# Low parts of the gated unit's activations by a negative copy and an accumulating transfer, and the phases' negated sine taken into a VectorE product

## The chip, the cores and the metric

One core of a Trainium2 chip. The time is device microseconds of one launch. The kernel before was timed in three runs, 730.05 to 732.71 us, median 732.13. Beside these stands one profiled execution, which has the rows quoted here.

Engines: TensorE (PE; its weight loads are PEld), VectorE (DVE), ScalarE (ACT), GpSimd (POOL) and SyncE (SP, which issues transfers). Each runs its own list of instructions in order and waits for the others by semaphores.

## The reference

```python
xn = _layernorm(x)                                  # x: 1 x 2048 x 448
# A: long convolution with a kernel made from the state space
A = -exp(log_A_real) + 1j * A_imag                  # 448 x 256
P = exp((A * dt)[:, :, None] * pos)                 # pos = 0 .. 2047
K = 2.0 * einsum("dn,dnl->dl", C * dt, P).real
y = irfft(rfft(xn, 4096) * rfft(K, 4096)) + xn * D_skip
# B: gated unit
h = sigmoid(xn @ w_gate) * (xn @ w_up)              # 2048 x 1792
out = x + y + h @ w_down
```

## The kernel before

Two generators write the program side by side: `conv()` (the convolution) and `glu()` (the gated unit). A loop at the end of the kernel takes the next piece of whichever is less far along by weights written beside the pieces; a scheduler then settles each engine's order from its own estimate of when each instruction can start, and `tc.high_priority` draws some forward.

**The gated unit.** Products are made in pieces of reduced precision: each operand is a high part and a low part, and three products (high x high, high x low, low x high) give one. `gate` (L694) makes 128 of the 1792 hidden columns for 512 tokens: 11 matmuls into each of two banks `gu` (gate and up), Tanh on ScalarE (`th`, L715), `hf = (th + 1) * up` on VectorE (L718), then the high part `hh` as a cast on ScalarE (L723) and the low part `hl = hf - hh` on VectorE (L725). `hf` has one buffer, `hh` and `hl` six each. After a group of two or three such column blocks, for two blocks of 512 tokens each, the down products `po` (L819) run over the group: `hh x dh`, `hh x dl`, `hl x dh` for each block of columns, nine matmuls a bank in a group of three, and VectorE adds the bank to `acc` (L824).

**The chunks.** `kgen` (L454) makes the convolution's kernel in 56 chunks of 8 channels. The 2048 positions are written as 64 coarse by 32 fine steps, so that the sum over the 256 states becomes a matmul of `Et` (64 steps) and `Ft` (32 steps). For a chunk:

- `ahead` (L527): TensorE makes the phases of both in the bank `tr` (L534); ScalarE makes `S` from it: Abs (L542), Sin (L543), the negated Sin of the coarse half (L544), and the cosines from Abs (L545). The five planes of `S` are sin, cos, -sin of the coarse steps, cos, sin of the fine steps. `S` has two buffers.
- `magnitudes` (L489), once for two chunks: GpSimd makes the powers `me` and `mf` by doubling (L500, L512), 11 products one after the other, in two buffers that VectorE frees.
- VectorE: the upper half of `Et` (L599) from cos and sin, the lower half (L600) from cos and -sin in reversed order, as the mirrored phases, and `Ft` (L601). `Et` has two buffers, `Ft` one.
- TensorE: 32 matmuls into the bank `ko` (L615). After four chunks it is copied to `ks`, and `first_stage` (L548) begins its transform.

GpSimd also makes low parts of down weights (`dl`, L789), and towards the end of the chunks begins transfers of weights (L641, L649).

Of the kernel before, what the change touches and what calls it, by code (L numbers as in the profile page):

```python
# [21 lines left out]
N = 256  # L22
# [4 lines left out]
TWO_PI = 2.0 * math.pi  # L27
# [103 lines left out]
def s4d_glu_kernel(ctx, tc, io):  # L131
# [322 lines left out]
    def kgen(pk):  # L454
# [4 lines left out]
            ("me1", [128, 4 * DC, 64], F32), ("mf1", [128, 4 * DC, 32], F32),  # L459
            ("S1", [128, 5, 2 * DC, 32], F32), ("Et1", [128, 2, 2 * DC, 64], F32),  # L460
            ("Et0", [128, 2, 2 * DC, 64], F32), ("Ft", [128, 2, 2 * DC, 32], F32),
            ("S0", [128, 5, 2 * DC, 32], F32), ("mf0", [128, 4 * DC, 32], F32),
            ("me0", [128, 4 * DC, 64], F32), ("pm0", [128, 12, NCH * 2 * DC], F32),
            ("ph0", [128, 2, N], F32R), ("ph1", [128, 2, N], F32R),
        ]
        tl = {n: pk.tile(sh, dt_, name=n) for n, sh, dt_ in late}


# [58 lines left out]
        def ahead(cn):  # L527


            S = tl[f"S{cn % 2}"]  # L530
            ps = psc[-1].tile([128, 2, 512], F32, name="tr", bufs=1)
            ph = pht[cn // 2 % 2]
            for h in range(2):
                nc.tensor.matmul(  # L534
                    ps[:, h], ph[:, cn % 2, 128 * h : 128 * h + 128], sel, start=True, stop=True
                )
            if cn % 2 == 1 and cn + 3 < NCK:
                phase_load(cn // 2 + 2)
            rows = lambda t: t.rearrange("p c (h e) s -> p h c (e s)", h=2)
            pv = ps.rearrange("p h (c x) -> p h c x", c=2)  # L540
            cs = S[:, 1:4:2]
            nc.scalar.activation(rows(cs), pv, AF.Abs)  # L542
            nc.scalar.activation(rows(S[:, 0:5:4]), pv, AF.Sin, scale=TWO_PI)  # L543
            nc.scalar.activation(rows(S[:, 2:3]), pv[:, :, 0:1], AF.Sin, scale=-TWO_PI)  # L544
            sins[:] = [nc.scalar.activation(cs, cs, AF.Sin, scale=-TWO_PI, bias=hpi)]  # L545
            return S
# [32 lines left out]
        for g in range(NCK // NCH):  # L579
            for c in range(NCH):  # L580
# [18 lines left out]
                v.tensor_tensor(Et[:, :, :, 32:64], two(me[:, :, 32:64]), S[:, 1::-1], ALU.mult)  # L599
                v.tensor_tensor(Et[:, :, :, 0:32], two(me[:, :, 0:32]), S[:, 1:3, :, ::-1], ALU.mult)  # L600
                fts[:] = [v.tensor_tensor(Ft, two(mf), S[:, 3:5], ALU.mult)]  # L601
                if cn + 2 < NCK and c % 2 == 0:
# [43 lines left out]
    def rd_load(f, rd=None, eng=nc.sync):  # L646
        if rd is None:
            rd = pg.tile([128, D], F32, name="rd", bufs=RB)
        eng.dma_start(rd, io["B_w_down"][128 * f : 128 * f + 128])  # L649
        return rd  # L650

    def w_low():
# [41 lines left out]
    def gate(w, xs, to, between=None):  # L694
# [29 lines left out]
        with hp(HP):  # L724
            v.tensor_tensor(hl, hf, hh, ALU.subtract)  # L725
        to.append((hh, hl))
# [307 lines left out]
    def conv():  # L1034
        with tc.tile_pool(name="psk", bufs=1, space=PSUM) as ps_, tc.tile_pool(
# [89 lines left out]
    xq, psc, raws, acl, marks, slots, pqs = list(x_first), [], [], [], [None, None], {}, []  # L1125
    W1s, GGs, act = [], [], []
    gens = [conv(), glu()]
# [42 lines left out]
```

## Time and profile before

| what | us |
|---|---|
| median of the three runs | 732.13 (730.05 to 732.71) |
| the profiled execution: its own time | 725.02 |
| its span, first to last instruction | 723.2 |
| TensorE busy in the span | 676.3 (94%) |
| VectorE busy | 565.1 (78%) |
| ScalarE busy | 420.8 (58%) |
| GpSimd busy | 384.5 (53%) |
| `hl` on VectorE (L725), 56 of them | 51.8 |
| lower half of `Et` on VectorE (L600), 56 | 79.5 |
| negated Sin on ScalarE (L544), 56 | 34.1 |
| cast `hh` on ScalarE (L723), 56 | 35.0 |

A grouped row reads: line, engine, operation, out<-in, shapes, count | busy us in all, mean ns of one | idle us of the engine just before them, and which work ended it. A row of stretches gives for each engine the busy time in it, with the instructions in brackets, then the granted clock of TensorE, the mean busy share of the DMA engines and GB/s. A row of waits reads: who <- for whom: us in all, times, the longest. A row of the order of time reads: start, us, engine, line, operation and in brackets the idle time ahead of it. TensorE's matmuls overlap, so its busy time counts some filling and is not a measure of its peak.

### The profile page before, as it was taken

What the parts mean: (1) busy time and instruction counts of PE and PEld (TensorE: products, weight loads), DVE (VectorE), ACT (ScalarE), POOL (GpSimd) and SP (SyncE); (2) the same over time, 40 slices, a digit from 0 to 9 for tenths busy, and PEclk for the clock granted to TensorE, in tenths of its full rate; (3) what the DMA queues carried; (4) which work ended last, traced back from release to release, by engine and by line L of the source; (5) the groups of instructions that cost most, each with busy time, mean ns of one, the idle gap of its engine ahead of it and who ended that gap; (6) DMA issues with size and microseconds to landing.
All of it is one profiled execution on the core that took longest, in us unless ns stands there. A gap on an engine that the chain in (4) does not pass through costs nothing.

```text
span 723.2 us, 19101 instructions
## 1 busy us (share of the span) xinstructions
PE 676.3 (94%) x7780; PEld 532.4 (74%) x7780; DVE 565.1 (78%) x776; ACT 420.8 (58%) x650; POOL 384.5 (53%) x430
## 2 busy tenths in 40 slices
PE   2998799997998999998999999999999999999996
PEld 1765688786886888655778887888877787777784
DVE  5799996799989999999588988987865555565543
ACT  3646364678687788898398687776742222322320
POOL 2120027699888788789556865776855001441004
PEclk9998999999999999999999999999999999999999
DMA  9946328434414545364853232232269999999745
GB/s 205 232 111 189 94 84 266 159 107 165 151 52 135 187 136 170 106 184 140 255 159 136 61 137 97 69 111 69 74 156 250 278 235 239 247 261 238 177 128 154
DMA packets 92823, 115.72 MB, mean 160 GB/s; under 512 B 12432, under 2 KB 81200, under 8 KB 92480
## 3 DMA queue, kind: packets, MB, share of 16 engines
q1 hardware_dynamic: 83328, 94.03, 47.5%
q10 hardware_dynamic: 6704, 14.51, 6.3%
q0 software_dynamic: 2704, 5.96, 3.4%
q8 instruction: 61, 1.00, 0.6%
q14 instruction: 26, 0.21, 0.1%
HBM read 69.70 MB, written 44.76 MB: 158 GB/s over the span
## 4 chain that ended last, share of the span: by engine, by line
PE 62%; DVE 16%; ACT 8%; DMA 7%; issue 4%; SPq 2%; POOL 1%; ACTq 0%; DVEq 0%; POOLq 0%
PE gu L707 24%; PE po L819 15%; PE sp L905 7%; PE ko L615 6%; PE pv L932 4%; PE tr L534 3%; DVE Et L600 2%; DVE Ft L601 2%; DVE Et L599 2%; DVE hl L725 1%; DMA acc_d<-acc 1%; DVE pm L448 1%; ACT S L545 1%; DMA xe<-in_A_u_dram 1%; DVE wl L762 1%
## 5 line engine op out<-in xcount | busy, mean ns | idle before, releaser
L512 POOL TENSOR_TENSOR me<-me,pm 128x32 f32<-128x32 f32 (+1 forms) x168 | 146.1, 870 | 83.5 <-DVE Et L600 70.8
L512 POOL TENSOR_TENSOR mf<-mf,pm 128x64 f32<-128x64 f32 (+1 forms) x112 | 120.7, 1078 | 4.9
L707 PE MATMUL gu<-xh,wh 128*128 128x512 f32 x336 | 100.7, 406 | 1.4 <-ACT xh L220 1.4
L707 PE MATMUL gu<-xh,wl 128*128 128x512 f32 x336 | 95.4, 391 | 0.0
L707 PE MATMUL gu<-xl,wh 128*128 128x512 f32 x336 | 95.1, 390 | 0.0
L819 PE MATMUL po<-dh,hh 128*128 128x448 f32 x224 | 85.7, 383 | 6.7 <-DVE xr L224 2.6
L599 DVE TENSOR_TENSOR Et<-me,S 128x1024 f32<-128x1024 f32 x56 | 81.7, 1460 | 9.5 <-ACT S L545 7.6
L600 DVE TENSOR_TENSOR Et<-me,S 128x1024 f32<-128x1024 f32 x56 | 79.5, 1419 | 8.4 <-ACT me L525 8.4
L601 DVE TENSOR_TENSOR Ft<-mf,S 128x1024 f32<-128x1024 f32 x56 | 79.4, 1418 | 7.4 <-ACT S L545 4.4
L819 PE MATMUL po<-dl,hh 128*128 128x448 f32 x224 | 83.6, 373 | 0.0
L819 PE MATMUL po<-dh,hl 128*128 128x448 f32 x224 | 82.7, 370 | 0.0
L542 ACT ACTIVATE S<-tr 128x1024 f32<-128x1024 f32 x56 | 57.8, 1032 | 39.7 <-PE tr L534 34.8
L707 PEld LDWEIGHTS gu<-xh,wh 128*128 128x128 f32 x336 | 61.9, 192 | 20.1 <-issue 4.8
L723 ACT CAST hh<-hf 128x512 fp32r<-128x512 f32 x56 | 35.0, 626 | 70.4 <-DVE hf L718 59.4
L615 PEld LDWEIGHTS ko<-Et,Ft 128*32 128x32 f32 x3584 | 55.2, 113 | 26.5 <-issue 16.3
L707 PEld LDWEIGHTS gu<-xh,wl 128*128 128x128 f32 x336 | 62.8, 188 | 14.9 <-DVE pl L308 0.7
L707 PEld LDWEIGHTS gu<-xl,wh 128*128 128x128 f32 x336 | 63.0, 188 | 14.0 <-issue 0.7
L615 PE MATMUL ko<-Et,Ft 128*32 128x64 f32 x3584 | 65.5, 225 | 8.1 <-DVE Et L599 4.6
L718 DVE SCALAR_TENSOR_TENSOR hf<-th,gu 128x512 f32<-128x512 f32 x56 | 38.1, 680 | 37.3 <-PE gu L707 27.8
L545 ACT ACTIVATE S<-S,hpi 128x1024 f32<-128x1024 f32 x56 | 65.5, 1170 | 0.0
L824 DVE SCALAR_TENSOR_TENSOR acc<-po,acc 128x448 f32<-128x448 f32 x80 | 48.4, 615 | 20.0 <-PE po L819 19.9
L725 DVE TENSOR_TENSOR hl<-hf,hh 128x512 fp32r<-128x512 f32 x56 | 51.8, 925 | 12.5 <-ACT hh L723 12.5
(196 smaller groups left out, 1286.4 us busy)
## 6 DMA issues: line engine op xcount, KB each, us to landing
sk_d<-sk ACTq DMA_DIRECT2D x14, 512.0 KB
sx<-x_d SPq DMA_DIRECT2D x32, 224.0 KB
skl<-sk_d SPq DMA_DIRECT2D x16, 448.0 KB
vp<-v_d SPq DMA_DIRECT2D x16, 448.0 KB
v_d<-vt SPq DMA_DIRECT2D x62, 112.0 KB
wt_d<-wh SPq DMA_DIRECT2D x9, 512.0 KB
wt_d<-wl SPq DMA_DIRECT2D x9, 512.0 KB
wl<-wt_d SPq DMA_DIRECT2D x9, 512.0 KB
```

The lines of the kernel that those rows point to most:

```text
L512: ins = nc.gpsimd.tensor_tensor(m[:, :, w + a : 2 * w : n], m[:, :, a:w:n], par(base + i).unsqueeze(2).to_broadcast([128, 4 * DC, w // n]) ...
L542: nc.scalar.activation(rows(cs), pv, AF.Abs)
L545: sins[:] = [nc.scalar.activation(cs, cs, AF.Sin, scale=-TWO_PI, bias=hpi)]
L599: v.tensor_tensor(Et[:, :, :, 32:64], two(me[:, :, 32:64]), S[:, 1::-1], ALU.mult)
L600: v.tensor_tensor(Et[:, :, :, 0:32], two(me[:, :, 0:32]), S[:, 1:3, :, ::-1], ALU.mult)
L601: fts[:] = [v.tensor_tensor(Ft, two(mf), S[:, 3:5], ALU.mult)]
L615: nc.tensor.matmul(ko[32 * j : 32 * j + 32, sl], Ft[:, cc, DC * h + 4 * q + j], Et[:, cc, DC * h + 4 * q + j], start=(k == 0), stop=(k == ...
L707: glu_mm[:] = [nc.tensor.matmul(ps, a_, b_, start=(n == 0), stop=(n == len(mm) - 1))]
L725: v.tensor_tensor(hl, hf, hh, ALU.subtract)
L819: glu_mm[:] = [nc.tensor.matmul(po, a_[:, bs], w_, start=(n == 0), stop=(n == 3 * fc - 1))]
L824: v.scalar_tensor_tensor(acc[:, b], po, 0.5, acc[:, b], ALU.mult, ALU.add)
L905: mm = nc.tensor.matmul(to, tb[:kk, t, 64 * c : 64 * c + 64], rhs, start=True, stop=True, skip_group_check=True,)
```

## The change

Two edits, both of the chunk stage.

**Low parts.** A new function `low` makes `hl` as ScalarE's copy of `hh` times -1, and GpSimd then issues a transfer from `hf` into `hl` that adds: `hl = -hh + hf`. While `kgen` runs (its tile `hf1` is put in the list `hfx`, which is emptied behind it) the gated unit takes this way, for 35 of its 56 blocks; the 21 others keep the subtraction. `hf` then alternates between its own buffer and `hf1`, since the transfer reads it later than VectorE did.

**Phases.** `S` has four planes instead of five: sin, cos of the coarse steps, cos, sin of the fine ones. ScalarE's negated Sin is gone. The lower half of `Et` becomes two instructions of half the size: one product with cos, and one scalar_tensor_tensor, `(me * -1) * sin`.

```diff
-            ("S1", [128, 5, 2 * DC, 32], F32), ("Et1", [128, 2, 2 * DC, 64], F32),
+            ("S1", [128, 4, 2 * DC, 32], F32), ("Et1", [128, 2, 2 * DC, 64], F32),
...
-            ("ph0", [128, 2, N], F32R), ("ph1", [128, 2, N], F32R),
+            ("ph0", [128, 2, N], F32R), ("ph1", [128, 2, N], F32R), ("hf1", [128, 512], F32),
         ]
         tl = {n: pk.tile(sh, dt_, name=n) for n, sh, dt_ in late}
+        hfx.append(tl["hf1"])
...
-            cs = S[:, 1:4:2]
+            cs = S[:, 1:3]
             nc.scalar.activation(rows(cs), pv, AF.Abs)
-            nc.scalar.activation(rows(S[:, 0:5:4]), pv, AF.Sin, scale=TWO_PI)
-            nc.scalar.activation(rows(S[:, 2:3]), pv[:, :, 0:1], AF.Sin, scale=-TWO_PI)
+            nc.scalar.activation(rows(S[:, 0:4:3]), pv, AF.Sin, scale=TWO_PI)
...
-                v.tensor_tensor(Et[:, :, :, 0:32], two(me[:, :, 0:32]), S[:, 1:3, :, ::-1], ALU.mult)
-                fts[:] = [v.tensor_tensor(Ft, two(mf), S[:, 3:5], ALU.mult)]
+                v.tensor_tensor(Et[:, 0, :, 0:32], me[:, :, 0:32], S[:, 1, :, ::-1], ALU.mult)
+                v.scalar_tensor_tensor(Et[:, 1, :, 0:32], me[:, :, 0:32], -1.0, S[:, 0, :, ::-1], ALU.mult, ALU.mult)
+                fts[:] = [v.tensor_tensor(Ft, two(mf), S[:, 2:4], ALU.mult)]
...
+    def low(lo, hi, full):
+
+        nc.scalar.activation(lo, hi, AF.Identity, scale=-1.0)
+        nc.gpsimd.dma_start(lo, full, accum_op=ALU.add)
...
-        hf = pg.tile([128, 512], F32, name="hf", bufs=1)
+        if hfx and len(hfs) % 2:
+            hf = hfx[0]
+        else:
+            hf = pg.tile([128, 512], F32, name="hf", bufs=1)
...
-            v.tensor_tensor(hl, hf, hh, ALU.subtract)
+            if not hfx:
+                v.tensor_tensor(hl, hf, hh, ALU.subtract)
+            else:
+                low(hl, hh, hf)
...
                 yield from kgen(pk)
+                hfx.clear()
```

The scheduler's order shifts with it. In the rows below L599 to L601 are lines of before; after the change `hf` is L727, `Ft` L602, the halves of the lower `Et` L600 and L601, the chunk product L616, the down product L831, GpSimd's products L513 and L501, and the transfer L656.

VectorE at a pair of chunks about a quarter of the way through, before (`hf` and `gu` belong to the gated unit, `pm` are powers for later chunks):

```order
L599 TENSOR_TENSOR Et_1125<-me_1122,S_1124 128x32x32
L600 TENSOR_TENSOR Et_1125<-me_1122,S_1124 128x32x32
L725 TENSOR_TENSOR hl<-hf,hh 128x512
L601 TENSOR_TENSOR Ft<-mf_1123,S_1124 128x1024
L448 SCALAR_TENSOR_TENSOR pm_1180<-pm_1180 128x128
L718 SCALAR_TENSOR_TENSOR hf<-th,gu 128x512
```

and of the change, from the same place:

```order
L600 TENSOR_TENSOR Et_1125<-me_1122,S_1124 128x16x32
L727 SCALAR_TENSOR_TENSOR hf_1134<-th,gu 128x512
L774 TENSOR_TENSOR wl<-wraw,wh 128x1024
L602 TENSOR_TENSOR Ft<-mf_1123,S_1124 128x1024
L448 SCALAR_TENSOR_TENSOR pm_1180<-pm_1180 128x128
L727 SCALAR_TENSOR_TENSOR hf<-th,gu 128x512
L600 TENSOR_TENSOR Et_1126<-me_1130,S_1128 128x16x32
L601 SCALAR_TENSOR_TENSOR Et_1126<-me_1130,S_1128 128x16x32
L599 TENSOR_TENSOR Et_1126<-me_1130,S_1128 128x32x32
```

The subtraction between the products is gone, the lower half of `Et` stands as two rows, and `hf` alternates between `hf` and `hf_1134`, which is `hf1`.

TensorE at the head of that group's down products, before (`po_2962` is the first bank; `ko` with `Et1` is the second chunk of the pair):

```order
L819 MATMUL po_2962<-dh_2832,hl_2825 128x448
L819 MATMUL po_2987<-dh_2401,hh_2393 128x448
...
L819 MATMUL po_3012<-dl_2404,hh_2393 128x448
L615 MATMUL ko_2445<-Et1_1125,Ft_1127 32x64 x32
L625 MATMUL ko_2445<-dm_79,ident_69 128x8
L534 MATMUL tr_2797<-sel_76,ph0_1132 128x512 x2
L819 MATMUL po_3012<-dh_2401,hl_2394 128x448
```

and of the change:

```order
L616 MATMUL ko_2449<-Et1_1125,Ft_1127 32x64 x32
...
L831 MATMUL po_2968<-dl_2840,hh_2828 128x448
L831 MATMUL po_2992<-dh_2405,hh_2396 128x448
L616 MATMUL ko_2870<-Et0_1126,Ft_1127 32x64 x32
L535 MATMUL tr_2904<-sel_76,ph1_1133 128x512 x2
L831 MATMUL po_2968<-dh_2837,hl_2829 128x448
L831 MATMUL po_2992<-dl_2408,hh_2396 128x448
```

The same chunk's product has moved ahead of the whole group of down products, the next chunk's is in among the first of them, and the first use of the last `hl` stands behind it. From chunk 27 of 56 on both orders have nearly the same work of the gated unit behind them again at the same chunk.

GpSimd in the second half of the chunks, of the change (`me1` and `mf1` are the magnitudes of a pair of chunks, `hf_5605` and `hf1_1134` the two blocks of tokens of the group's last columns):

```order
L513 TENSOR_TENSOR mf1_1123<-mf1_1123,pm1_1180 128x32x4
L513 TENSOR_TENSOR me1_1122<-me1_1122,pm1_1180 128x32x16
L513 TENSOR_TENSOR mf1_1123<-mf1_1123,pm1_1180 128x32x8
L513 TENSOR_TENSOR mf1_1123<-mf1_1123,pm1_1180 128x32x16
L656 DMA hl_5608<-hf_5605 128x512
L656 DMA hl_5693<-hf1_1134 128x512
L513 TENSOR_TENSOR me0_1130<-me0_1130,pm0_1131 128x32
```

and TensorE where the first of the two is used:

```order
L616 MATMUL ko_5334<-Et1_1125,Ft_1127 32x64 x32
L626 MATMUL ko_5334<-dm_79,ident_69 128x8
L535 MATMUL tr_5667<-sel_76,ph0_1132 128x512 x2
L713 MATMUL gu_5677<-xh_3868,wh_5497 128x512 x3
...
L831 MATMUL po_5767<-dh_5388,hh_5383 128x448
L831 MATMUL po_5712<-dh_5612,hl_5608 128x448
L616 MATMUL ko_5723<-Et0_1126,Ft_1127 32x64 x32
```

Both transfers stand behind all 11 products of the pair's magnitudes; before, the next chain followed there at once. Between the chunk product `ko_5334` and the first use of `hl_5608` TensorE has the last half of a gate and 12 down products.

More of the change, by code (lines that the diff above doesn't have):

```diff
@@ L459, in kgen @@
             ("me1", [128, 4 * DC, 64], F32), ("mf1", [128, 4 * DC, 32], F32),
-            ("S1", [128, 5, 2 * DC, 32], F32), ("Et1", [128, 2, 2 * DC, 64], F32),
+            ("S1", [128, 4, 2 * DC, 32], F32), ("Et1", [128, 2, 2 * DC, 64], F32),
             ("Et0", [128, 2, 2 * DC, 64], F32), ("Ft", [128, 2, 2 * DC, 32], F32),
-            ("S0", [128, 5, 2 * DC, 32], F32), ("mf0", [128, 4 * DC, 32], F32),
+            ("S0", [128, 4, 2 * DC, 32], F32), ("mf0", [128, 4 * DC, 32], F32),
             ("me0", [128, 4 * DC, 64], F32), ("pm0", [128, 12, NCH * 2 * DC], F32),
-            ("ph0", [128, 2, N], F32R), ("ph1", [128, 2, N], F32R),
+            ("ph0", [128, 2, N], F32R), ("ph1", [128, 2, N], F32R), ("hf1", [128, 512], F32),
         ]
         tl = {n: pk.tile(sh, dt_, name=n) for n, sh, dt_ in late}
+        hfx.append(tl["hf1"])
         pms = [tl["pm0"]]
@@ L1125, in s4d_glu_kernel @@
     xq, psc, raws, acl, marks, slots, pqs = list(x_first), [], [], [], [None, None], {}, []
-    W1s, GGs, act = [], [], []
+    W1s, GGs, act, hfx = [], [], [], []
     gens = [conv(), glu()]
```

## The prediction

> **What bounds the kernel now.** I read the run's span and clock first, then the busy time of the engines by stage, then the grouped rows of VectorE inside the stage that the change touches, then the waits of that stage. The change lies between about 143 and 536 us, where the 56 chunks of the convolution kernel are made beside the gated unit. I cut that stage in two where the picture changes:
>
> ```profile
> core 0: 723.2 us, clock 0.984
> ...
> core 0: us, PE busy (x) PEld busy (x) DVE busy (x) ACT busy (x) POOL busy (x), PEclk, DMA share, GB/s
> 143.00:338.00 195.00, 183.21 (x2753) 143.02 (x2751) 185.43 (x190) 158.41 (x238) 165.79 (x163) 0.97 0.43 136
> 338.00:536.00 198.00, 195.16 (x2957) 159.58 (x2960) 162.71 (x171) 139.76 (x202) 134.82 (x156) 1.00 0.41 126
> ```
>
> In the first stretch VectorE is busy for 185.4 of 195 us, 95%, the highest share of any engine, and TensorE has 11.8 us of idle time. In the second TensorE is busy for 195.2 of 198 us and VectorE has 35 us to spare. So work taken from VectorE can only be worth something in the first stretch, and there never more than TensorE's 11.8 us; in the second TensorE sets the pace, and anything that it waits for is lost in full. What VectorE does in the first stretch, and who waits for it:
>
> ```profile
> L600 DVE TENSOR_TENSOR Et<-me,S 128x1024 f32<-128x1024 f32 x28 | 41.6, 1488 | 2.5 <-ACT me L525 2.5
> L601 DVE TENSOR_TENSOR Ft<-mf,S 128x1024 f32<-128x1024 f32 x27 | 40.4, 1498 | 0.1
> L599 DVE TENSOR_TENSOR Et<-me,S 128x1024 f32<-128x1024 f32 x27 | 39.0, 1443 | 3.7 <-ACT me L525 1.9 <-ACT S L545 1.8
> L725 DVE TENSOR_TENSOR hl<-hf,hh 128x512 fp32r<-128x512 f32 x16 | 18.1, 1128 | 0.0
> ...
> PE ko L615 <- DVE Et L599: 4.6, 2, 2.9
> ...
> PE ko L615 <- DVE Ft L601: 2.5, 3, 1.9
> ```
>
> The three products of a chunk take 121 us of the 185, the 16 subtractions that make low parts take 18.1. TensorE's waits in the chunks' own products are for Et and Ft, as they must be if VectorE paces the stretch.
>
> **The change part by part.** *Low parts leave VectorE.* In the chunks 35 subtractions `hl` go, 16 of them in the first stretch: 18.1 us off VectorE there. *The split of one product.* L600 becomes two instructions of 512 elements, one of them a scalar_tensor_tensor. Neither form, with both inputs in SBUF, stands in the trace; the nearest rows bound them:
>
> ```profile
> L600 DVE TENSOR_TENSOR Et<-me,S x56: 1208/1222/2175, 139.1 to 530.4; 128x1024 f32<-128x1024 f32 x56
> L725 DVE TENSOR_TENSOR hl<-hf,hh x56: 623/692/2662, 29.8 to 691.3; 128x512 fp32r<-128x512 f32 x56
> L718 DVE SCALAR_TENSOR_TENSOR hf<-th,gu x56: 628/680/689, 27.5 to 689.9; 128x512 f32<-128x512 f32 x56
> L544 ACT ACTIVATE S<-tr x56: 592/605/670, 135.7 to 527.6; 128x512 f32<-128x512 f32 x56
> L723 ACT CAST hh<-hf x56: 603/621/690, 28.2 to 690.6; 128x512 fp32r<-128x512 f32 x56
> ```
>
> (The three numbers are the least, the median and the most, in ns.) Two halves at the medians, 692 + 680 = 1372 ns against 1222, cost 0.15 us more a chunk: the low end. If each half met what a subtraction met in this stretch, 2 x 1128 against 1488, it is 0.77 us: the high end. A 1024-element product here has a mean 0.27 us above its median, so an operation more should meet about that much more: I take 0.15 + 0.27 = 0.42 us, which lies between. Over 28 chunks that is 11.8 us (ends 4.2 and 21.6). VectorE's net in the first stretch is 11.8 - 18.1 = -6.3 us (ends -13.9 and +3.5).
>
> *ScalarE.* It loses L544, 28 x 0.605 = 16.9 us in the first stretch, and gains 16 negative copies, priced by the cast of the same shape at 0.62 us: 9.9. Net -7 us of its 158. VectorE's idle time put down to ScalarE in the rows above is 2.5 + 3.7 = 6.2 us; ends are nothing and all of it, and I take a third, -2, because most of it is behind the squares (L525), which the change leaves as they are.
>
> *What of it reaches the time.* VectorE's 8.3 us: ends are none (TensorE takes over) and all of it. I take 0.8, because TensorE's 11.8 us of idle time must also cover its waits for ScalarE and the late operands below: -6.6 us. The program's new order fits this. It places chunk products ahead of the down products of their group, so VectorE is asked for Et and Ft earlier and TensorE's other work fills the end of the stretch; the work itself is the same.
>
> *The transfers.* Each is issued by GpSimd, in order, between the magnitude products. Their price on GpSimd is that of its other issues; how long one takes to land is not in the trace for a transfer within SBUF that adds, so the nearest rows bound it:
>
> ```profile
> L643 POOL DMA_DIRECT2D wraw<-in_B_w_up_dram x10 | 5.3, 530 | 0.0
> L641 POOL DMA_DIRECT2D wraw<-in_B_w_gate_dram x5 | 3.9, 788 | 2.0 <-POOL dl L796 1.2 <-ACT x L690 0.8
> ```
> ```profile
> rdw<-in_B_w_down_dram POOLq DMA_DIRECT2D x5, 224.0 KB, 5.2
> ...
> sel<-in_c_sel_dram POOLq DMA_DIRECT2D x1, 256.0 KB, 11.3
> ...
> bk<-in_c_bk_dram POOLq DMA_DIRECT2D x1, 128.0 KB, 2.3
> ```
> ```profile
> POOL me L512 <- DVE Et L600: 22.9, 11, 3.3
> ```
> The first two rows are issues (the last number before the bar is the mean ns on GpSimd), the next three transfers with KB and median us to landing, the last GpSimd's wait in the first stretch.
>
> 16 issues at 0.53 to 0.79 us put 8 to 13 us on GpSimd in the first stretch. It is busy for 165.8 of 195 and waits 22.9 us for VectorE to free `me`: the issues fit into that wait, so I cost them at nothing; with that cover gone they would push each magnitude chain by one or two issues, 1.2 us a pair of chunks. For landing I take 4 us (256 KB, DMA half idle in these stretches by the 0.43 and 0.41 above): between 128 KB in 2.3 and 224 KB in 5.2, with 11.3 for 256 KB in the crowded start as the far end. The Trainium skill, "DMA: Bandwidth & Descriptors", section "Anatomy of one DMA — SWDGE (gpsimd) path", fits 2.0 us plus bytes over 436e3: an estimate by that page is 2.6 us for 256 KB, and by it the late operand below would be 1.4 us cheaper; no run here shows it yet.
>
> *Where an operand comes too late.* What is queued behind the waiting instruction: a transfer stands behind a whole magnitude chain on GpSimd, and TensorE's down product that needs `hl` stops everything behind it. The place shown in the part on the change (`hl_5608`) has its counterpart of before here, GpSimd's chain and the chunk product that ends its pair:
>
> ```profile
> 450.24 2.08 POOL L512 TENSOR_TENSOR me<-me,pm 128x32 f32<-128x32 f32 x3 [5.67 <-DVE Et L600]
> ...
> 456.85 3.62 POOL L512 TENSOR_TENSOR mf<-mf,pm 128x256 f32<-128x256 f32 x2
> ```
>
> TensorE at the same time, and below it two merged rows of the chain of waits for the pace of its products:
>
> ```profile
> 454.36 1.10 PE L615 MATMUL ko<-Et,Ft 128*32 128x64 f32 x64
> 455.39 0.39 PE L625 MATMUL ko<-dm,ident 128*128 128x8 f32 x2
> ...
> 456.19 0.85 PE L707 MATMUL gu<-xh,wh 128*128 128x512 f32 x3
> ```
> ```profile
> 394.72 4.87 PE po L819 x24
> ...
> 422.76 2.49 PE gu L707 x11
> ```
>
> The chain ends at 456.85 + 3.62 = 460.5, 6.1 us after that ko began, and the transfer would land 4 us later, at +10.1. TensorE, from the ko to the first use: 1.8 us to the gate (454.36 to 456.19), 2.5 for its 11 products, 12 down products at 4.87/24 = 0.20: +6.7. So the operand is 3.4 us late, in the stretch where TensorE is full. The same count at the other heads of groups there gives 0 and 0.7 us late. I take +3 us (ends 0, if VectorE runs further ahead and the chain starts sooner, and +7 with a landing of 5.2 at all three). Two such heads lie in the first stretch, 1 to 3 us late each; that is in the 0.8.
>
> **Sum.** -6.6 + 3.0 = -3.6 us on the profiled execution, whose span is 723.2 and whose time is 725.0: 721.4. The runs shown lie higher (median 732.1), so on them I forecast 732.13 - 3.64 = 728.5, given as **728**. Nothing before 143 us or after 536 us changes but by the shift.
>
> **Rivals.**
> (1) *Transfers land late* (slower). One mechanism: `hl` is ready only after the chain on GpSimd and a slow landing, and TensorE stops at the head of each group. It decides from a landing of about 5 us, where the slack of the other heads is used up. With 7 us each of three heads in the second stretch loses 3 more, +9, and the two in the first about 3 each beyond their cover, +6: -3.6 + 15 = +11.4, 743. For it: GpSimd's 11.3 us row, and VectorE operations drawn out from 692 to 2662 ns beside GpSimd's, so one holds the other up. Against it: the DMA share of 0.4 here.
> The Trainium skill, "SBUF — State Buffer", section "A bandwidth-pool intuition that's wrong (but worth ruling out)", says that a transfer issued by GpSimd waits for its descriptors while VectorE holds the shared port, 3100 ns where 620 would do. By that an estimate of the landing here is 2.5 us longer, which is this rival; the trace of before shows no such transfer beside a chunk, so it speaks neither way.
> (2) *The split eats the relief* (slower). Both halves meet GpSimd's products as a subtraction does: VectorE +3.5 us, nothing back from ScalarE, +3 for the late head: +6.5, 738.6. For it: the mean of 1128 against the median of 692 in just this stretch. Against it: GpSimd has only so many products to get in the way with.
> (3) *More comes back*. Halves at their medians, -13.9, and ScalarE's 6.2: more than TensorE's idle time, so -11.8 + 0 for the head: 720.
> (4) *It does nothing that shows*: TensorE has no room even in the first stretch, the head is in time: 732.
>
> **Chances.** Forecast 0.38 (its own range 724 to 732, so about 0.28 of it is faster and 0.10 not told from before), (1) 0.23, (2) 0.20 (0.03 of it in the middle), (3) 0.17, (4) 0.02. About 0.5%, 3.7 us, is what a measurement of this kernel can tell from no change. Faster 0.28 + 0.17 = 0.45; same 0.10 + 0.03 + 0.02 = 0.15; slower 0.23 + 0.17 = 0.40. The range runs from a little below (3) to a little above (1): 717 to 746.
>
> **What would show it.** VectorE's group of `hl` falls to 21 and the halves of Et come out at 0.7 to 1.1 us each; the stretch up to the 28th chunk is 5 to 8 us shorter with VectorE still at 95%; L544 is gone. Wrong: TensorE waiting for `hl` by DMA at `po` for more than 5 us in all (rival 1); halves that sum to 1.9 us or more (rival 2); transfers landing in 3 us or less and the second stretch no longer at all (rival 3); GpSimd's wait for Et gone and Et waiting for GpSimd's `me`, which no case above has.

## The result and the profile after

The changed kernel takes 757.46 us (median of four runs, 756.78 to 758.02) against 731.09 for the kernel before, timed beside it (four runs, 726.04 to 732.71). The ratio is 1.0372, with a 95% interval of 1.0319 to 1.0426: slower, by 26 us. The profiled execution took 757.68 us. The first rows of its page, span and TensorE's busy time:

```profile
span 755.8 us, 19190 instructions
...
PE 688.9 (91%) x7780; PEld 540.3 (71%) x7780; DVE 554.0 (73%) x797; ACT 415.2 (55%) x629; POOL 372.9 (49%) x465
```

TensorE runs the same 7780 instructions as before, so its busy time should have stayed at 676.3 us. It grew by 12.6, and the time that it was not busy by 20.0: together the 32.6 us by which the span is longer. (The profiled execution of before, 725.0 us, is one of its quickest, so this is some 6 us more than the 26 of the medians.) The 12.6 us go with the clock. The mean granted clock fell from 0.984 to 0.968, and (1 - 0.968) x 755.8 = 24.2 us of lost clock against (1 - 0.984) x 723.2 = 11.6 before is the same 12.6; part of the slow clock falls where TensorE stands anyway, so that the two agree to the tenth is chance. So there are two things to find: new idle time of TensorE, and a lower clock that comes with it.

The two stretches of the chunks, as they were cut for the prediction (columns as there):

```profile
core 0: us, PE busy (x) PEld busy (x) DVE busy (x) ACT busy (x) POOL busy (x), PEclk, DMA share, GB/s
143.00:338.00 195.00, 180.64 (x2669) 140.37 (x2668) 177.47 (x194) 147.88 (x214) 157.72 (x175) 0.96 0.53 151
338.00:536.00 198.00, 186.73 (x2700) 151.33 (x2700) 139.78 (x168) 133.41 (x190) 120.82 (x167) 0.97 0.49 136
```

Now no engine is full in either: VectorE has gone from 185.4 to 177.5 us of the first 195, and TensorE from 195.2 to 186.7 of the second 198, with 257 instructions fewer done in it. All engines idle more, which means that they wait for each other. The halves of the lower `Et` (L600, L601) and the new transfers, in the grouped rows of VectorE and of GpSimd:

```profile
L601 DVE SCALAR_TENSOR_TENSOR Et<-me,S 128x512 f32<-128x512 f32 x56 | 51.0, 910 | 10.2 <-ACT S L544 9.7 <-POOL mf L513 0.5
L600 DVE TENSOR_TENSOR Et<-me,S 128x512 f32<-128x512 f32 x56 | 50.8, 907 | 22.8 <-ACT me L526 21.1 <-PE ko L616 1.0 <-POOL mf L501 0.5
```
```profile
L656 POOL DMA_DIRECT2D hl<-hf x35 | 31.1, 888 | 51.1 <-ACT hl L655 42.8 <-ACT xh L220 8.3
```

The split costs 907 + 910 - 1419 = 398 ns a chunk. An issue holds GpSimd for 0.89 us, and ahead of the issues GpSimd stood still for 51.1 us, 42.8 of them because it takes its list in order and the negative copy that the transfer adds to was not there yet. Who waits for whom, after and then before (us in all, times, the longest):

```profile
POOL hl L656 <- ACT hl L655: 42.8, 11, 9.7
...
POOL me L513 <- DVE Et L600: 39.6, 10, 9.2
...
PE po L831 <- DMA hl<-hf: 11.8, 5, 4.5
...
POOL me L513 <- DVE Et L601: 8.3, 1, 8.3
```
```profile
POOL me L512 <- DVE Et L600: 70.8, 23, 11.4
...
PE ko L615 <- DVE Et L599: 4.6, 2, 2.9
...
PE ko L615 <- DVE Ft L601: 3.2, 4, 1.9
```

GpSimd's wait for VectorE, which was to hide the issues, is down from 70.8 to 39.6 + 8.3 = 47.9 us, and TensorE has a wait that the kernel before cannot have: 11.8 us for `hl` by DMA, in five stops: 1.0 us at 134.7 us, 0.4 and 3.2 in the first stretch, 2.6 and 4.5 in the second. The longest of them is the place that the prediction counted out (`hl_5608`). GpSimd and TensorE there, in the order of time:

```profile
463.96 2.07 POOL L513 TENSOR_TENSOR me<-me,pm 128x32 f32<-128x32 f32 x3 [3.26 <-DVE Et L600]
...
470.01 3.62 POOL L513 TENSOR_TENSOR mf<-mf,pm 128x256 f32<-128x256 f32 x2
473.57 0.86 POOL L656 DMA_DIRECT2D hl<-hf  x1
```
```profile
468.57 1.10 PE L616 MATMUL ko<-Et,Ft 128*32 128x64 f32 x64
...
475.15 0.37 PE L831 MATMUL po<-dh,hh 128*128 128x448 f32 x1
480.05 0.74 PE L831 MATMUL po<-dh,hl 128*128 128x448 f32 x1 [4.54 <-DMA hl<-hf]
480.72 1.94 PE L616 MATMUL ko<-Et,Ft 128*32 128x64 f32 x64
```

The magnitude chain runs to 473.6, the transfer is issued behind it, and TensorE, done with what stands ahead at 475.5, stands for 4.54 us. The forecast and the find can be compared term by term, from the start of the `ko` at 468.57: the chain ends at +5.1 us where +6.1 was forecast, and the landing takes 480.0 - 473.6 = 6.4 us where 4 was. Then look at the two `ko`: the same 64 matmuls take 1.10 us ahead of the stop and 1.94 behind it. Stretches around it:

```profile
core 0: us, PE busy (x) PEld busy (x) DVE busy (x) ACT busy (x) POOL busy (x), PEclk, DMA share, GB/s
468.00:475.00 7.00, 7.00 (x93) 5.83 (x92) 6.96 (x8) 5.75 (x8) 6.35 (x5) 1.00 0.30 95
475.00:480.00 5.00, 0.52 (x3) 0.14 (x1) 2.03 (x3) 1.25 (x2) 2.49 (x5) 0.82 0.89 210
480.00:485.00 5.00, 4.95 (x71) 4.09 (x72) 1.85 (x2) 1.15 (x2) 0.97 (x3) 0.50 0.05 10
485.00:490.00 5.00, 5.00 (x84) 4.37 (x83) 3.30 (x5) 2.83 (x4) 3.32 (x5) 1.00 0.00 2
```

The clock is granted at 0.50 after the stop and is whole again by 485. This stop is paid twice: once standing, once at half speed. From 475 to 480 the DMA engines were busy at 0.89, against the mean of 0.41 of this stretch in the kernel before, on which the 4 us rested. A busy VectorE need not draw a landing out: it was busy for 3.4 of these 6.4 us, and a transfer issued at 533.9 us landed in 3.3 with VectorE busy throughout and the DMA engines at 0.46. Two transfers of 35 are no rule.

### The profile page after: what moved, and what is told of

It is laid out like the page before. It is cut to its first block, busy times and chain, and to the rows that moved or that the text cites. A ratio compares the mean times of both kernels' runs of the same rounds, so it can differ in the third digit from the quotient of the medians.

```text
span 755.8 us, 19190 instructions
## 1 busy us (share of the span) xinstructions
PE 688.9 (91%) x7780; PEld 540.3 (71%) x7780; DVE 554.0 (73%) x797; ACT 415.2 (55%) x629; POOL 372.9 (49%) x465
## 3 DMA queue, kind: packets, MB, share of 16 engines
q0 software_dynamic: 7744, 15.14, 10.1%
## 4 chain that ended last, share of the span: by engine, by line
PE 44%; DVE 13%; DMA 8%; ACT 7%; issue 5%; POOL 4%; SPq 2%; ACTq 1%; POOLq 0%; DVEq 0%
PE gu L713 15%; PE po L831 10%; PE sp L917 6%; PE ko L616 4%; PE pv L944 3%; DVE Ft L602 3%; DVE Et L599 3%; PE tr L535 2%; DMA hl<-hf 2%; POOL me L513 2%; DVE Et L601 2%; DMA ac<-acc_d 1%; DVE Et L600 1%; POOL mf L513 1%; ACT S L543 1%
## 5 line engine op out<-in xcount | busy, mean ns | idle before, releaser
L513 POOL TENSOR_TENSOR me<-me,pm 128x32 f32<-128x32 f32 (+1 forms) x168 | 135.2, 805 | 63.4 <-DVE Et L600 39.6
L513 POOL TENSOR_TENSOR mf<-mf,pm 128x64 f32<-128x64 f32 (+1 forms) x112 | 108.0, 965 | 4.7
L831 PE MATMUL po<-dh,hl 128*128 128x448 f32 x224 | 85.4, 384 | 11.8 <-DMA hl<-hf 11.8
L831 PE MATMUL po<-dh,hh 128*128 128x448 f32 x224 | 87.6, 391 | 5.1 <-DVE acc L836 2.5
L831 PE MATMUL po<-dl,hh 128*128 128x448 f32 x224 | 86.2, 385 | 0.0
L602 DVE TENSOR_TENSOR Ft<-mf,S 128x1024 f32<-128x1024 f32 x56 | 80.5, 1437 | 5.8 <-PE ko L616 4.8
L599 DVE TENSOR_TENSOR Et<-me,S 128x1024 f32<-128x1024 f32 x56 | 81.2, 1450 | 0.5 <-ACT S L545 0.3
L616 PEld LDWEIGHTS ko<-Et,Ft 128*32 128x32 f32 x3584 | 55.5, 113 | 29.8 <-issue 15.9
L616 PE MATMUL ko<-Et,Ft 128*32 128x64 f32 x3584 | 65.7, 225 | 10.9 <-DVE Ft L602 5.2
L713 PEld LDWEIGHTS gu<-xl,wh 128*128 128x128 f32 x336 | 64.0, 191 | 14.3 <-issue 0.7
L727 DVE SCALAR_TENSOR_TENSOR hf<-th,gu 128x512 f32<-128x512 f32 x56 | 38.1, 680 | 41.8 <-PE gu L713 30.5
L600 DVE TENSOR_TENSOR Et<-me,S 128x512 f32<-128x512 f32 x56 | 50.8, 907 | 22.8 <-ACT me L526 21.1
L601 DVE SCALAR_TENSOR_TENSOR Et<-me,S 128x512 f32<-128x512 f32 x56 | 51.0, 910 | 10.2 <-ACT S L544 9.7
```

Of the source, the lines that this page charges most:

```text
L513: ins = nc.gpsimd.tensor_tensor(m[:, :, w + a : 2 * w : n], m[:, :, a:w:n], par(base + i).unsqueeze(2).to_broadcast([128, 4 * DC, w // n]) ...
L600: v.tensor_tensor(Et[:, 0, :, 0:32], me[:, :, 0:32], S[:, 1, :, ::-1], ALU.mult)
L601: v.scalar_tensor_tensor(Et[:, 1, :, 0:32], me[:, :, 0:32], -1.0, S[:, 0, :, ::-1], ALU.mult, ALU.mult)
L602: fts[:] = [v.tensor_tensor(Ft, two(mf), S[:, 2:4], ALU.mult)]
L616: nc.tensor.matmul(ko[32 * j : 32 * j + 32, sl], Ft[:, cc, DC * h + 4 * q + j], Et[:, cc, DC * h + 4 * q + j], start=(k == 0), stop=(k == ...
L713: glu_mm[:] = [nc.tensor.matmul(ps, a_, b_, start=(n == 0), stop=(n == len(mm) - 1))]
```

## Experiments

Each run was timed against the kernel before on the same chip; its median there was 728.8 to 730.8 us. The ratios' intervals are about 0.3 to 0.6% to either side, 2 to 4 us.

| kernel | median us | ratio, 95% interval |
|---|---|---|
| phases' part alone (`phases_only`) | 746.8 | 1.0230 [1.0171, 1.0289] |
| transfers' part alone (`low_only`) | 747.2 | 1.0221 [1.0169, 1.0274] |
| change, heads of groups by subtraction (`last_sub`) | 754.7 | 1.0314 [1.0250, 1.0378] |
| change without transfers (`no_transfer`) | 743.9 | 1.0181 [1.0124, 1.0239] |
| change in the order of before (`after_in_before`) | 741.9 | 1.0175 [1.0117, 1.0233] |
| before in the order of the change (`before_in_after`) | 745.4 | 1.0236 [1.0177, 1.0296] |
| phases alone, order of before | 730.6 | 1.0023 [0.9991, 1.0054] |
| transfers alone, order of before | 751.2 | 1.0307 [1.0263, 1.0352] |
| heads by subtraction, order of before | 730.9 | 0.9998 [0.9966, 1.0031] |
| no transfers, order of before | 719.8 | 0.9854 [0.9801, 0.9906] |
| transfers issued earlier, order of before | 732.7 | 1.0029 [0.9994, 1.0064] |
| transfers without phases, heads by subtraction, order of before | 737.0 | 1.0109 [1.0074, 1.0144] |
| change, TensorE alone in the order of before | 752.6 | 1.0309 [1.0256, 1.0361] |
| before, TensorE alone in the order of the change | 743.0 | 1.0183 [1.0126, 1.0241] |
| transfers that nobody waits for, order of before | 728.0 | 0.9979 [0.9948, 1.0011] |
| heads by subtraction and early issue, order of before | 732.1 | 1.0038 [1.0012, 1.0064] |
| subtraction on GpSimd, order of before | 737.6 | 1.0119 [1.0087, 1.0151] |
| the same, heads on VectorE | 733.5 | 1.0049 [1.0021, 1.0078] |

**The two parts apart.** The theories at this point were: T1, late operands and the half clock behind each stop; T2, the split eats VectorE's relief (the prediction's second rival); T3, the scheduler's new order; T4, GpSimd blocked at the issues. The first run is the change with `hfx` left empty; the second has the five planes and the whole L600 back, and writes `hf` over `th`:

```diff
-        hfx.append(tl["hf1"])
```
```diff
+            nc.scalar.activation(rows(S[:, 2:3]), pv[:, :, 0:1], AF.Sin, scale=-TWO_PI)
...
+        th = pg.tile([128, 512], F32, name="th", bufs=2)
...
+        hf = th
```

> The four planes and the split product alone; every low part is VectorE's subtraction as before. Theory T1 (the transfers make TensorE wait for hl, and each such stall is followed by a stretch at half clock): near the kernel before, 728 to 736 us, since ScalarE loses about 34 us and VectorE gains about 22 us, and no operand comes by DMA. Rival T2 (the split eats VectorE's relief): most of the 26 us are here, 745 us or more, because VectorE has the 22 us of the split without the relief. T3 (the scheduler's new order): anything, told by where the chunks stand.

> The transfers alone, with five planes, the negated Sin and the whole lower product of before; hf is written over th, which has two buffers. T1: still slow, 748 to 760 us, with TensorE waiting more than 8 us for hl by DMA and more half-clock windows than the 6 of before. T2: faster than before, 718 to 728 us, since VectorE is relieved of 40 us and pays nothing.

Measured: 746.8 and 747.2 us. Each part alone loses 16 us. That fits no theory whole: T1 does not have the first, T2 not the second, and in the second TensorE waited for `hl` for 5.1 us, not for more than 8. In the first, where nothing comes by DMA, TensorE's waits for `Ft` had risen from the 3.2 us above:

```profile
PE ko L615 <- DVE Ft L601: 11.2, 9, 4.1
```

**Transfers at the heads, and transfers at all.** The third kernel keeps the subtraction for the last column block of each group, the fourth drops the transfer:

```diff
-            if not hfx:
+            if not hfx or last:
                 v.tensor_tensor(hl, hf, hh, ALU.subtract)
...
-                    yield from gate(ws[f - f0], xq[2 * half + t], hs[t], between)
+                    yield from gate(ws[f - f0], xq[2 * half + t], hs[t], between, f == fs_[-1])
```
```diff
-        nc.gpsimd.dma_start(lo, full, accum_op=ALU.add)
```

> As the change, but the last column block of each group keeps VectorE's subtraction: 22 transfers in place of 35, none of which is needed soon after its issue. T1: TensorE's wait for hl by DMA falls below 3 us, and with its share of the half clock 10 to 20 us come back: 737 to 748 us. T2: no gain, 755 to 762 us, VectorE has 13 subtractions more. T4 (GpSimd, blocked in order at the issue until ScalarE's negative copy is done, delays the magnitudes): a gain in proportion to the transfers left out, a third of the 26 us, 748 us, with the waits of TensorE for Et falling and not those for hl.

> As the change without the transfer: hl is the negative copy alone, the addition of hf is left out, and with it GpSimd's issue and the landing. T1 and T4 both: all of what the transfers cost comes back, 720 to 733 us. T2: 745 us or more, since VectorE's work is as in the change. T1 and T4 are told apart by the run that keeps 22 transfers and by the waits for hl there.

Measured: 754.7 and 743.9 us. In the third no wait for `hl` by DMA was left, and hardly any time came back: TensorE waited 11.1 us for `Ft` instead. Without any transfer 13 us are still lost. Three of the four lose 13 to 17 us and the third 24, whatever is taken out. What all four share is an order that the scheduler has made anew; whether that is the cause, the next runs ask.

**Orders held.** So the order was taken out of the scheduler's hands. A table lists the instructions of an engine, as numbers in the order of the source text, in the order in which another kernel's engine has them; each gets an edge to the one ahead of it, which holds the issue and waits for nothing:

```python
for p, i in zip(order, order[1:]):
    tc.add_manual_dep(
        i, p.name,
        mybir.DependencyInfo(mybir.DependencyClass.NoSync, mybir.DependencyReason.DATA),
        reason="pin",
    )
```

TensorE's instructions are the same, one for one, in both kernels; on the other engines those that only one of them has are placed as the expectations say. Four kernels: the two kernels in each other's order, and each part in the order of before.

> The whole change, but the compute instructions of TensorE, VectorE, ScalarE and GpSimd are held in the order of the kernel before: the second half product right behind the first, the negative copy right behind its cast, the transfers placed by the scheduler between GpSimd's products. Theory O (the two edits cost little by themselves; what costs is that the scheduler, given other instructions, places the chunks otherwise, so that TensorE stops more often, each longer stop with its half clock): 725 to 738 us. Rival C (the edits' own work costs: split, blocked GpSimd, landing): 745 us or more, with TensorE's wait for hl by DMA still above 8 us.

> The mirror: the kernel before, all of its work unchanged, held in the order that the changed kernel has on the four engines; the 35 subtractions and the 56 negated Sins, which the changed kernel has not, are placed by the scheduler. Theory O: 745 to 758 us, though not one operation has changed. Rival C: 728 to 736 us, as before.

> The phases' part alone (four planes, split product, all low parts by subtraction) in the order of the kernel before; it was 746.8 us in the order that the scheduler gave it. Theory O: 728 to 737 us, since VectorE pays about 12 us of the split in the first stretch, where TensorE has 11.8 us of idle time and ScalarE is relieved. Rival C: 744 us or more, VectorE being the bound up to the 28th chunk.

> The transfers alone (five planes, whole product, hf written over th) in the order of the kernel before; it was 747.2 us in the scheduler's own. Theory O: 722 to 733 us, VectorE being relieved where it is the bound. Rival C: 742 us or more, with TensorE waiting for hl by DMA for more than 5 us.

Measured: 741.9, 745.4, 730.6 and 751.2 us. The first falls between the two expectations, the fourth into that of rival C. The second is the telling one: the kernel before, with not one operation changed, loses 14.7 us by the medians (2.4% by the ratio, 17 us) when it is held in the order of the changed kernel. The third is its counterpart: the phases' part, 16 us slower as scheduled, cannot be told from the kernel before in the old order. T2 falls with it. The kernel before was not held in its own order, but the edges by themselves can cost little: with them this run is at 730.6 us, and one further down at 719.8. The transfers keep a cost of their own, 11 us with the phases' part and 20 without. (The kernel without it has no `hf1`, so there ScalarE's next Tanh waits until the transfer has read `th`, 11.5 us in all.) The mirror's waits, and stretches around its longest stop for `Ft`:

```profile
PE ko L615 <- DVE Ft L601: 12.8, 10, 3.8
```
```profile
core 0: us, PE busy (x) PEld busy (x) DVE busy (x) ACT busy (x) POOL busy (x), PEclk, DMA share, GB/s
365.00:370.00 5.00, 5.00 (x82) 3.98 (x81) 2.45 (x2) 3.57 (x6) 2.83 (x6) 1.00 1.01 283
370.00:380.00 10.00, 6.17 (x66) 4.92 (x68) 3.89 (x7) 3.62 (x6) 0.00 (x0) 0.91 0.77 231
380.00:385.00 5.00, 5.00 (x75) 3.70 (x70) 4.10 (x5) 2.26 (x4) 1.59 (x2) 0.50 0.65 210
```

Chunk products that stand earlier in TensorE's list meet `Ft` too soon: 12.8 us of waiting for it in place of 3.2, and half a clock behind the long stops. In the change held in the old order TensorE waits 6.0 us for `Et`, near the 4.6 of before; what remains is the wait for the transfers, as long as in the scheduler's own order:

```profile
PE po L831 <- DMA hl<-hf: 11.9, 5, 4.4
```

So in the change the order does not cost by the mirror's wait for `Ft` alone. The profiled executions, scheduled and held, differ by 755.8 - 739.4 = 16.4 us of span. TensorE's busy time has 7.1 of it (688.9 against 681.8, at a clock of 0.968 against 0.975), its waits for `Et` and `Ft` 3.6 (10.3 against 6.7); the rest is spread over waits of 3 us and less.

**What of the transfers costs, in the order of before.** Heads by subtraction; no transfers; transfers moved ahead on GpSimd (`_LOWS` holds the transfers, `_AT` the place of each among GpSimd's products, read from the trace of the whole change in the order of before); and the heads by subtraction without the phases' part.

```diff
+        if engine == "Pool":
+            for n, t in reversed(list(zip(_AT, _LOWS))):
+                order.insert(n, t)
```

> The change in the order of the kernel before, but the last column block of each group keeps VectorE's subtraction: 22 transfers in place of 35. In that order all 35 cost 11.1 us, with 12.5 us of stops of TensorE for hl at five heads of groups. Theory H (the late operand at the heads is all of that cost): no stop for hl by DMA of a microsecond or more, 722 to 733 us. Rival Q (the issues and the blocked GpSimd cost, wherever the operand is used): two thirds of the cost stay, 736 to 740 us.

> The change in the order of the kernel before without any transfer: the addition of hf is left out. Theory H: 722 to 731 us, like the run that keeps 22 transfers. Rival Q: 4 us or more below that run. Rival N (the negative copy on ScalarE itself delays the chunks): stays at 736 us or more.

> The change in the order of the kernel before, each transfer placed on GpSimd behind those magnitude products that had begun when its negative copy ended, 2 to 4 products earlier for the most part. Theory H with the queue as its cause: the stops for hl fall from 12.5 us below 5 and the time by about as much with the half clock, to 730 to 735 us. If the landing of 4.4 us is the cause and not the queue, 739 us or more; if GpSimd is then blocked at the issue, TensorE's waits for Et grow instead.

> Only transfers that are not needed soon: the low parts of all blocks but the last of a group by negative copy and transfer, with the five planes and the whole product of before, in the order of before; hf is written over th. Theory H: VectorE is relieved of about 10 subtractions where it is the bound and nothing is late: 718 to 729 us, the one that may beat both kernels. Rival Q: 732 us or more.

Measured: 730.9, 719.8, 732.7 and 737.0 us. Without transfers the change gains 11 us: VectorE's and ScalarE's relief is real. Its stretches, where VectorE is as full as before and TensorE does 97 instructions more in the first:

```profile
143.00:338.00 195.00, 188.45 (x2850) 145.75 (x2849) 185.51 (x211) 158.46 (x232) 161.16 (x168) 0.99 0.45 145
338.00:536.00 198.00, 194.59 (x2989) 160.90 (x2989) 148.43 (x171) 136.41 (x190) 121.08 (x155) 1.00 0.38 120
```

Issuing the transfers two to four products earlier takes 9 us off the 741.9, and TensorE's wait for `hl` falls from 11.9 to 2.9 us: most of the late operand was the place behind the chain, as expected of the queue. That it ends no better than before, and that 22 uncritical transfers end level too, suggests that the transfers also cost where nobody waits; the 13 subtractions that come back to VectorE are the rival for the 22, and the next runs ask. The fourth missed its expectation by 8 us: without the phases' part ScalarE keeps the negated Sin beside the negative copies, and TensorE waited 7.4 us for the copy `ks` on ScalarE, where the kernel before has 3.1. Shared `th` and `hf` play a part too: ScalarE stood for 12.2 us in six waits until a transfer had read `th`. How much of the 8 us is theirs was not tried.

**Which engine's order, and what an issue costs by itself.** The change with TensorE alone in the old order, the kernel before with TensorE alone in the new one, 35 transfers that nobody waits for (without the addition, as at 719.8 us), and the heads' subtraction together with the early issue. The third:

```diff
         nc.scalar.activation(lo, hi, AF.Identity, scale=-1.0)
+        nc.gpsimd.dma_start(io["scr"][len(hfs) - 1], full)
```

> The whole change with TensorE alone held in the order of the kernel before; VectorE, ScalarE and GpSimd as the scheduler places them around it. With all four engines held it was 741.9 us, with none 757.5. Theory P (TensorE's order is what moves the time, the others follow it): 739 to 746 us. Theory V (the order on VectorE, ScalarE and GpSimd matters, as when a subtraction, a product or a cast stands before or behind the one that TensorE waits for): 749 us or more.

> The mirror: the kernel before with TensorE alone in the order of the changed kernel. With all four engines held in that order it was 745.4 us. Theory P: 741 to 749 us. Theory V: 728 to 737 us.

> The run without transfers in the order of before (719.8 us), with 35 transfers of hf to DRAM added on GpSimd that nothing waits for but the next use of hf: the issues and the traffic without the late operand. The addition of hf to hl is left out here too. Theory H (only the late operand costs): 718 to 723 us. Rival Q (the issues, and GpSimd blocked until hf is there, delay the magnitudes): 726 us or more, 4 us and up being half of what the run with 22 transfers lost.

> The change in the order of before with 22 transfers (the last block of a group by subtraction; that was 730.9 us), and these placed earlier on GpSimd as in the run that had all 35 so. If what is left of the transfers' cost is their place between the magnitude products: 722 to 728 us, faster than both kernels. If it is the 13 subtractions that stay on VectorE: 729 to 733 us, no change.

Measured: 752.6, 743.0, 728.0 and 732.1 us. In the kernel before, TensorE's order, with the other engines placed around it by the scheduler, brings most of the loss, 13.4 us, and the same wait for `Ft` (12.6 us). Here theory P holds. In the change it does not: with TensorE held and the rest left to the scheduler the wait for `Ft` is down to 2.1 us, from 5.2, and a longer one for the transfers has come:

```profile
PE po L831 <- DMA hl<-hf: 20.1, 6, 5.0
```

The orders of TensorE and GpSimd belong together: move one alone and the operand is late on the other. The transfers that nobody waits for cost 8 us by the medians (728.0 against 719.8; by the ratios 0.9979 - 0.9854 = 1.25%, 9 us). They go to DRAM and wait for `hf`, not for the negative copy, so this is a measure of issues and traffic, not an exact share. GpSimd's wait for VectorE shows where it goes, without transfers and with those:

```profile
POOL me L513 <- DVE Et L601: 83.8, 24, 13.9
```
```profile
POOL me L513 <- DVE Et L601: 53.2, 23, 4.6
```

30 us of GpSimd's slack are used up by 35 issues. The last run brought nothing over 730.9, as expected if the 13 subtractions on VectorE are what is left.

**No landing at all.** GpSimd subtracts by itself at the places of the early transfers, once all 35, once all but the heads:

```diff
-        nc.scalar.activation(lo, hi, AF.Identity, scale=-1.0)
-        nc.gpsimd.dma_start(lo, full, accum_op=ALU.add)
+        nc.gpsimd.tensor_tensor(lo, full, hi, ALU.subtract)
```

> The change in the order of before, with neither the negative copy nor the transfer: GpSimd itself subtracts (hl = hf - hh), at the places where the early transfers stood. If the landing after the issue is what makes the 35 transfers cost 8 to 22 us, a subtraction of 1 to 2 us in the place of an issue of 0.9 and a landing of 4.4 gives 722 to 729 us, faster than both kernels. If GpSimd's time and its hold on VectorE's products are what costs, 733 us or more.

> The same with the last block of each group by VectorE (22 subtractions on GpSimd, 13 more on VectorE). If late operands at the heads are still there in the run with 35: 2 to 5 us below that run. If not: the same or slower by up to 4 us, VectorE being the bound in the first stretch.

Measured: 737.6 and 733.5 us, both slower than before, the second by little. Grouped rows of the run with 35, VectorE's halves and GpSimd's subtractions:

```profile
L601 DVE SCALAR_TENSOR_TENSOR Et<-me,S 128x512 f32<-128x512 f32 x56 | 64.8, 1158 | 0.0
L600 DVE TENSOR_TENSOR Et<-me,S 128x512 f32<-128x512 f32 x56 | 61.7, 1101 | 1.2 <-ACT me L526 0.8
```
```profile
L655 POOL TENSOR_TENSOR hl<-hf,hh 128x512 fp32r<-128x512 f32 x35 | 56.4, 1611 | 10.1 <-ACT hh L731 10.1
```

A subtraction holds GpSimd for 1.61 us, twice an issue, and VectorE's halves are drawn out from 0.91 to 1.10 and 1.16 us beside it. TensorE's wait for `hl` in the run with 35 is only 2.2 us. So GpSimd's time and its hold on VectorE weigh more than the landing that is saved. No version tried that does all of the work beats the kernel before by more than the measurement can tell; the one that gains, 719.8 us, leaves out the addition.

## Why the prediction was wrong, point by point

The loss can be walked in four steps, each the difference of two ratios times 730.7 us, and each uncertain by some 4 to 6 us:

| step | ratio | us |
|---|---|---|
| the change without transfers, in the order of before | 1 to 0.9854 | -10.7 |
| 35 transfers that nobody waits for | to 0.9979 | +9.1 |
| their data waited for, as in the change | to 1.0175 | +14.3 |
| the scheduler's own order | to 1.0372 | +14.4 |

- *VectorE paces the first stretch, and relief there is worth something.* Right, and undersized: -6.6 was forecast, -10.7 came. That this is close to the 11.8 that the third rival named as the most is luck: TensorE's idle time in the first stretch fell from 11.8 to 6.5 us only, and the rest came elsewhere.
- *The split costs 0.42 us a chunk.* Right: 0.40. It could not be told in the time in the old order.
- *"The program's new order fits this ... the work itself is the same."* This is the step that failed. The order was read as harmless because it has the same work in it; it costs 14.7 us on the kernel before with nothing else changed, and 14.4 in the change. VectorE being asked for `Et` and `Ft` earlier was seen, and taken for a gain; in the kernel before it makes TensorE wait for `Ft` for 12.8 us where it was 3.2. In the change that wait is only 5.2, and the order is paid in more and smaller stops and in the clock behind them.
- *The issues on GpSimd cost nothing, hidden in its wait for `Et`.* Wrong. They took 0.89 us each, somewhat over the 0.53 to 0.79 of the rows used, and stood behind negative copies for 42.8 us more; 9 us reach the time even where no data is waited for. The prediction named the cover and the price without it, and did not see that an issue blocks GpSimd until its operand is there.
- *Landing 4 us.* Right in the median, 3.8, but 6.4 at the head that the prediction counted out, within 3.3 to 7.5:

```profile
DMA to landing us min/median/max: 3.3/3.8/7.5
```

  The 2.6 us that the Trainium skill's fit gave ("DMA: Bandwidth & Descriptors", section "Anatomy of one DMA — SWDGE (gpsimd) path") lies below the least of the 35; the measurement decides. That the trace of before shows no such transfer of GpSimd's beside a chunk was misread: six for weights, from DRAM, were issued from 349 to 353 us and landed in 5.7 to 9.6.
- *The late operand, +3 us.* The mechanism was right to the place: first use forecast at +6.7 from the `ko`, due at 475.15 + 0.20 - 468.57 = +6.8; operand at +10.1, found at 480.05 - 468.57 = +11.5. That the operand is off by 1.4 us only is in part luck, a chain 1 us early and a landing 2.4 late. The term was mis-sized: in the second stretch 2.62 + 4.54 = 7.2 us, a little above its far end of 7, and behind long stops comes the half clock, which the prediction left out although its own stretch rows showed a clock of 0.97. In the first stretch 3.7 us came, where 2 to 6 had been taken for covered. The walk puts wait and clock together at 14.3 us, near the 18 of the first rival's late heads (the 3, and 15 more). That rival's sign came (11.8 us of waiting for `hl`, against 5), the second's did not (halves of 1.82 us a chunk, against 1.9). But at 743 us the first rival still rests on the order being free, as every case of the prediction did; so all of them ended at least 14 us too low. That the change in the old order takes 741.9 us is near its 743 by other terms: it had the issues at nothing and less relief.

How the 14.4 us of order in the change divide among its engines and stops stays open: with TensorE alone put back 5 us return.

## What to carry to other kernels

Where a scheduler sets the order, an edit has two prices, that of its instructions and that of the order that it brings; hold the old order by edges, and hold the kernel before in the new one, and both can be measured apart, in two runs. An issue on an in-order engine costs until its operand is there, so price a transfer at the wait ahead of its issue, the place in the queue and the landing, and put it early or only where nobody waits soon. And price a stop of TensorE of two microseconds or more above its length, for the clock that can follow.

## What the runs showed of the hardware

Stops of TensorE of about two microseconds were followed by half the clock for 3.4 us, but not all of them. In the changed kernel, a stop of 1.90 us for `Ft` in the order of time, and stretches around it:

```profile
174.00 1.61 PE L616 MATMUL ko<-Et,Ft 128*32 128x64 f32 x64 [1.90 <-DVE Ft L602]
```

```profile
core 0: us, PE busy (x) PEld busy (x) DVE busy (x) ACT busy (x) POOL busy (x), PEclk, DMA share, GB/s
170.99:174.41 3.42, 1.52 (x50) 1.05 (x52) 3.39 (x4) 3.01 (x4) 3.34 (x3) 1.00 0.49 149
174.41:177.82 3.41, 3.41 (x95) 2.59 (x85) 3.41 (x5) 2.72 (x4) 3.25 (x3) 0.50 0.53 164
177.82:181.23 3.41, 3.18 (x38) 2.31 (x37) 3.41 (x3) 3.41 (x6) 3.41 (x6) 1.00 0.63 137
```

and in the change held in the order of before, around a stop of 2.08 us for `hl`, from 183.1 to 185.2:

```profile
180.32:183.73 3.41, 2.79 (x14) 2.13 (x12) 2.35 (x3) 3.41 (x6) 3.18 (x5) 1.00 1.07 315
183.73:187.15 3.42, 1.97 (x67) 1.61 (x68) 3.42 (x5) 1.56 (x3) 3.42 (x4) 1.00 0.88 298
187.15:190.56 3.41, 3.41 (x18) 3.14 (x17) 3.05 (x5) 3.17 (x4) 3.25 (x4) 1.00 0.30 86
```

The first loses 1.7 us of clock on top of its wait, the second nothing. The Trainium skill ("TensorE: Matmul & The Clock Gate", section "What's actually happening") has the clock halved after an idle window of about 3.4 us; these rows agree with the 3.4 us as the length of the slow stretch, and show that a shorter stop can bring it on.

What tells the two stops apart is where they lie. In each of the twenty traces of this case the granted clock changes only at times that lie whole multiples of 3.41 us apart. They cut the span into windows of 3.41 us, and the rows above are these windows. The first stop lies whole in one window, in which TensorE stands for 1.90 us, and the next window runs at half clock. The second, longer stop is cut at 183.73 into 0.6 and 1.45 us, and behind neither part the clock falls. From 130 to 700 us of the twenty traces all 60 windows at full clock in which TensorE stood for 1.8 us or more were followed by half clock; of some 180 with 0.7 to 1.8 us, 20 were, and five with less. So a little over half a window of standing was always enough here; what else counts is open. The windows do not start with the program: the first to end did so 0.4 us after its first instruction in the kernel before, 0.3 us in the change and 2.8 us in the change held in the old order. So the same stop of two microseconds may cost its clock in one execution and not in another.
